# Chunked attention into a SwiGLU layer on one core: the second tile's tokens turned by VectorE and DMA instead of TensorE, weight stores and a tile's loads moved, 16 small transposes added

## The chip, the cores and the metric

The kernel runs on one core of a Trainium2 chip. Its time is the device time of one launch in microseconds (us); the number compared is the median of several runs. The core has TensorE (PE in the rows, with PEld for its weight loads), VectorE (DVE), ScalarE (ACT), GpSimd (POOL) and SyncE (SP), which here issues nearly all of the DMAs, one after the other.

## The reference

What is computed, cut to its core: attention inside chunks of 64 tokens for 8 batches and 8 heads, then RMS norm and a SwiGLU layer over the 4608 tokens, all in float32.

```python
scores = scale * (q_c @ k_c.T)            # chunks of 64, head_dim 64
attn = softmax(scores)                    # exp(s - max) / (sum + 1e-9)
x = (attn @ v_c)  -> (4608, 512)          # heads side by side
xn = x / sqrt(mean(x * x) + 1e-6) * rms_g
g, val = xn @ w_gate, xn @ w_val          # 512 -> 1536
out = (g * sigmoid(g) * val) @ w_out      # 1536 -> 512
```

## The kernel before, in words

**Tiles.** The 4608 tokens are 9 tiles of 512 (TT), each of two units of 256 tokens. Tiles 0 to 2 (PLAIN = 3) are computed plainly, the loop `for t in range(PLAIN)`. The other six go two at a time through `up_pair` and `down_pair`, which use a scheme with seven products on sums of weight blocks. Every operand of a product is split into a high and a low part (fp32r), and three products are summed (high by high, high by low, low by high): `up` is 12 matmuls of 128x512 for a gate (ps_g) and 12 for a value (ps_v), `down` is 12 into four accumulators (acc).

**A plain tile.** For each of the 12 blocks f of the hidden width: `gate_and_value(f)` on TensorE, `gated` (Silu on ScalarE, the product on VectorE, then the high and low parts gh and gl), and the `down` of block f-1. At the end come `down` of the last block and `evacuate`, which stores four blocks of rows.

**Weights.** During tile 0 ScalarE and VectorE turn the weights from their stored form into high and low parts (`conv_step`, lines 191 to 243), 18 pieces in all. These parts are written back to DRAM for the later tiles: blocks that are stored as they are by `save_plain` (lines 687 and 742, three stores of 512 KB into wsd and three of 256 KB into osd for each of six i), and sums of blocks by `sides` (loads `w<-wfd` at line 754, sums on GpSimd at 749, splits and stores at 777 to 780).

**The tokens of a tile.** A unit passes scores, softmax, product with v, and the norm, and gives rows of tokens. The layer wants them with the model's width on the partitions. Units 0 and 1 (tile 0) are turned in the prelude by TensorE transposes (`x_turn_unit`, line 544). Units 2 and 3 (tile 1) are computed during t == 0 (`norm_unit`) and turned by `x_transpose` at line 533: 16 transposes of 128x128 on TensorE, eight ahead of the last but one `down` of tile 0 and eight ahead of the last. From unit 4 on there is another way: `turn_x` swaps 32x32 blocks within partitions on VectorE (STREAM_TRANSPOSE, line 458) and writes the result to DRAM (away_x, line 461), and `turn_x_back` reads it back in four DMAs (line 468) so that it lands turned; `x_split` then scales by g and makes the parts xh and xl.

**What sets the order.** In the prelude the order of TensorE, ScalarE and VectorE is that of the code (`manual_schedule`), and TensorE's is that of the code from t == 1 on. Everything else, SP's queue of DMAs among it, is ordered by a scheduler. Each engine works off its queue in order, so a DMA that waits holds up the ones behind it in SP's queue. The DMAs named below are `qt`, `kt`, `vt` (a unit's inputs), `away_e` and `eT` (a unit's attention weights, out to DRAM and back turned), `away_x` and `x`.

**Line numbers.** They are those of the kernel before; in the changed one the same lines stand a few numbers off.

Of the kernel before, what the change touches and what calls it, by code (L numbers as in the profile page):

```python
# [13 lines left out]
AF = mybir.ActivationFunctionType  # L14
ALU = mybir.AluOpType
AX = mybir.AxisListType

P = 128
# [67 lines left out]
def tile_chunk_attn_swiglu(  # L86
# [47 lines left out]
    def bank(pool, name):  # L134
        return pool.tile([P, 512], F32, tag=pool_tag[id(pool)], name=name)
# [358 lines left out]
        nc.scalar.activation(spent, xs, AF.Square, accum_out=ss)  # L494
        return root(ss, "ri")

    def norm_unit(u, banks):
        rs = state.pop(("rs", u))
        subs = [state.pop(2 * u + s) for s in range(2)]
        first = 2 * u % NSUB  # L500
        xu = x[:, first : first + 2]
        xv = xu.rearrange("p s (j b a d) -> p j s b a d", j=2, b=2, d=Q)
        for j in range(2):
            for b in range(2):
                nc.vector.tensor_tensor(
                    xv[:, j, :, b],
                    banks[j].rearrange("p s (a b d) -> p b s a d", b=2, d=Q)[:, b],
                    rs[:, :, :, j].broadcast_to([P, 2, NPAIR, Q]),
                    op=ALU.mult,
                )  # L510
        ss = small.tile([P, 2], F32, name="ss_u")
        for s, st in enumerate(subs):
            spent = st["e"].rearrange("p a j k -> p (a j k)")
            nc.scalar.activation(spent, xu[:, s], AF.Square, accum_out=ss[:, s : s + 1])
        ri = root(ss, "ri_u")
        for s in range(2):
            nc.gpsimd.tensor_scalar(xu[:, s], xu[:, s], ri[:, s : s + 1], None, op0=ALU.mult)

    def x_split(dt, pt, cols):
        g = g_col[:, dt : dt + 1]  # L520
# [5 lines left out]
            lo, pt, g, hi.bitcast(F32), op0=ALU.mult, op1=ALU.subtract  # L526
        )

    def x_transpose(dts):
        for dt in dts:  # L530
            pt = bank(ps_a, "ps_x")
            for s in range(NSUB):
                nc.tensor.transpose(
                    pt[:, s * P : (s + 1) * P], x[:, s, dt * P : (dt + 1) * P], ident
                )
            x_split(dt, pt, slice(0, TT))

    def x_turn_unit(u, d, pool):
        pt = state["xt", u, d] = bank(pool, "ps_x")
        for k in range(2):  # L540
            for s in range(2):
                at = (2 * k + s) * P
                src = x[:, 2 * u + s, (d + k) * P : (d + k + 1) * P]
                nc.tensor.transpose(pt[:, at : at + P], src, ident)
# [600 lines left out]
    with tc.manual_schedule(engines=FIRST_IN_ORDER):  # L1145
        for i, pool in enumerate((ps_a, ps_h)):
            scores(i, two_banks(pool, "ps_s"))
        softmax(0)
        softmax(1)
        att_transpose(0)  # L1150
        conv_abs(0)
        att_transpose(1)
        conv_low(0)
        softmax_sum(0)
        softmax_sum(1)
        conv_clamp(0)
        for i, pool in enumerate((ps_h, ps_acc)):
            att_values(i, two_banks(pool, "ps_o"))
            first_norm(i)
        first_squares(0)  # L1160
        first_root(0)
        for i, pool in ((2, ps_acc), (3, ps_h)):
            scores(i, two_banks(pool, "ps_s"))
        softmax(2)
        scale_one = first_scale(0, False)
        next(scale_one)
        softmax(3)
        att_transpose(2)
        conv_low(1)
        conv_load(AHEAD)  # L1170
        att_transpose(3)
        next(scale_one)
        conv_abs(1)
        softmax_sum(2)
        conv_shift(0)
        softmax_sum(3)
        for i in (2, 3):
            att_values(i, two_banks(ps_acc, "ps_o"))
            first_norm(i)
        first_squares(1)  # L1180
        first_root(1)
        for d in range(0, NDT, 2):
            x_turn_unit(0, d, ps_a)
        conv_sign(0)
        conv_cast(0)
        conv_clamp(1)
        conv_shift(1)
        conv_load(AHEAD + 1)
        for _ in first_scale(1, True):
            pass  # L1190
        conv_end(0)
        for d in range(0, NDT, 2):
            x_turn_unit(1, d, ps_acc)
        for d in range(0, NDT, 2):
            for u in range(2):
                x_high_unit(u, d)
        for d in range(0, NDT, 2):
            for u in range(2):
                x_low_unit(u, d)
        conv_sign(1)  # L1200
        conv_abs(2)
        conv_cast(1)
        conv_low(2)
        conv_clamp(2)
        conv_end(1)
        between = [
            lambda: conv_shift(2),
            lambda: conv_abs(3),
            lambda: conv_sign(2),
        ]  # L1210
        gs = {0: gated(0, (0, 1, 2), lambda: between.pop(0)())}
        ps = {1: gate_and_value(1)}
        conv_load(AHEAD + 2)
        conv_cast(2)
        conv_low(3)
        conv_clamp(3)
        conv_end(2)
        conv_shift(3)
        conv_sign(3)
    conv_at[0] = EARLY  # L1220

    for t in range(PLAIN):
        if t == 1:
            ordered = tc.manual_schedule(engines={mybir.EngineType.PE})
# [2 lines left out]
            for n, u in enumerate((4, 5)):  # L1227
                for k, f in enumerate(unit_steps(u, x)):
                    at.setdefault(2 + 9 * n + FIRST_STEPS[k], []).append(f)
            half = Steps(at)  # L1230
            st = last.open("st", 1)
            made = [[] for _ in range(NF + 2)]
# [5 lines left out]
        elif t == 2:  # L1238
# [2 lines left out]
            at = {}  # L1241
            for n, u in enumerate(range(2 * PLAIN, 2 * PLAIN + 4)):
                for k, f in enumerate(unit_steps(u, (x, x2)[n // 2])):
                    after_it = {1: LATE_STEPS, 2: LONG_STEPS}.get(n, UNIT_STEPS)
                    at.setdefault(max(UNIT_AT[n] + after_it[k], 0), []).append(f)
            for i in range(OUT_FIRST):
# [15 lines left out]
        for f in range(NF):  # L1262
            if f in gs:
                conv_step()
                g = gs.pop(f)
            else:
                g = gated(f, CONVS[f % 2], conv_step, ps.pop(f, None))
            if t == 0:
# [10 lines left out]
                elif f in (2, 7):  # L1279
                    for i in (2 * u, 2 * u + 1):  # L1280
                        att_transpose(i)
                elif f in (3, 8):
                    o = two_banks(ps_a, "ps_o")
                    for i in (2 * u, 2 * u + 1):
                        att_values(i, o)
                    norm_unit(u, o)
                if f == NF - 1:
                    x_transpose((0, 1))
            elif t == 1 and f == NF - 1:
                for dt in range(NDT):  # L1290
                    x_split(dt, blocks(x)[:, :, dt], slice(0, TT))
            if t == 1:
                if f % 2 == 0:
                    save_plain(f // 2)
                for todo in made.pop(0):
                    todo()
            if t:
# [3 lines left out]
            if t:  # L1301
                half()
            prev = g
        if t == 0:
            x_transpose((2, 3))
        down(acc, NF - 1, *prev)
        for s in range(NSUB):
            evacuate(acc, t, s)
# [84 lines left out]
```

## Time and profile before

| | |
|---|---|
| median of 3 runs | 898.38 us (897.68 to 898.59) |
| the profiled execution | 898.29 us, its span 896.5 us |
| TensorE busy | 880.0 us, 98% of the span |
| VectorE, ScalarE, GpSimd busy | 607.6, 454.1, 185.7 us (68%, 51%, 21%) |
| granted TensorE clock, mean | 0.991 of full |
| DMA | 231.84 MB, mean 259 GB/s |

The span runs from the first to the last instruction; 1.8 us of the execution lie around it. The prelude takes the first 27 us, tile 0 ends at about 138 us, tile 1 at 242 us and tile 2 at 352 us. Times in the rows are microseconds from the span's start.

### The profile page before, as it was taken

The numbers are of one execution on the slowest core, as the hardware profiler recorded it, in microseconds if no ns is written. First come the engines' busy times: TensorE is split into PE (matmuls) and PEld (weight loads), VectorE is DVE, ScalarE is ACT, GpSimd is POOL, SyncE is SP. The second block draws the span as 40 slices with busy tenths as digits, with TensorE's granted clock in tenths as the row PEclk, the third lists the DMA queues.
The fourth block names the chain that finished last, engine by engine and source line by source line (L and its number), as shares of the span: only waits on it lengthen the run. The fifth ranks groups of instructions, "written<-read, shape, count | busy, mean of one in ns | idle before, by whom it ended". The sixth has DMA issues, their size and how long they took to land.

```text
span 896.5 us, 17443 instructions
## 1 busy us (share of the span) xinstructions
PE 880.0 (98%) x6828; PEld 720.6 (80%) x6828; DVE 607.6 (68%) x965; ACT 454.1 (51%) x772; POOL 185.7 (21%) x157
## 2 busy tenths in 40 slices
PE   5999999999999999999999999999999999999998
PEld 4778888888888888888887888888878888888886
DVE  6999955364568745985677997556769953334776
ACT  5988934253446464454456645435547522222452
POOL 0004050342200000233233003333330014323200
PEclk8899999999999999999999999999999999999999
DMA  9889999777978855698977877677667794445442
GB/s 349 328 318 336 332 337 347 239 255 235 303 252 234 267 170 196 250 298 294 320 240 265 318 301 286 245 277 249 232 231 286 281 355 171 152 154 199 179 165 95
DMA packets 85794, 231.84 MB, mean 259 GB/s; under 512 B 8912, under 2 KB 45264, under 8 KB 71504
## 3 DMA queue, kind: packets, MB, share of 16 engines
q1 hardware_dynamic: 84656, 230.20, 73.1%
q8 instruction: 54, 0.88, 0.4%
q10 hardware_dynamic: 1056, 0.52, 0.2%
q14 instruction: 28, 0.23, 0.1%
HBM read 167.25 MB, written 63.44 MB: 257 GB/s over the span
## 4 chain that ended last, share of the span: by engine, by line
PE 94%; DVE 2%; ACT 2%; DMA 0%; issue 0%; POOL 0%; ACTq 0%; DVEq 0%
PE ps_b L857 11%; PE ps_a L857 11%; PE ps_c L857 11%; PE acc L664 11%; PE ps_g L627 11%; PE ps_v L627 10%; PE ps_b L1070 6%; PE ps_c L1070 6%; PE ps_d L857 5%; PE ps_a L1070 5%; PE ps_d L1070 3%; PE ps_o L426 2%; PE ps_s L299 2%; PE ps_o L484 1%; DMA x<-qT_dram 0%; ACT raw L196 0%
## 5 line engine op out<-in xcount | busy, mean ns | idle before, releaser
L857 PE MATMUL ps_b<-xp,wr 128*128 128x512 f32 x432 | 104.7, 391 | 0.1
L857 PE MATMUL ps_c<-xp,wr 128*128 128x512 f32 x432 | 104.0, 390 | 0.0
L857 PE MATMUL ps_a<-xp,wr 128*128 128x512 f32 x432 | 103.8, 390 | 0.0
L627 PE MATMUL ps_g<-xh,parts 128*128 128x512 f32 x288 | 97.2, 399 | 0.1
L857 PEld LDWEIGHTS ps_b<-xp,wr 128*128 128x128 f32 x432 | 80.5, 188 | 17.4 <-issue 0.5
L857 PEld LDWEIGHTS ps_c<-xp,wr 128*128 128x128 f32 x432 | 80.9, 188 | 16.9
L627 PE MATMUL ps_v<-xh,parts 128*128 128x512 f32 x288 | 94.5, 389 | 0.0
L857 PEld LDWEIGHTS ps_a<-xp,wr 128*128 128x128 f32 x432 | 80.8, 188 | 17.0
L664 PE MATMUL acc<-parts,gh 128*128 128x512 f32 x288 | 90.2, 394 | 0.0
L945 POOL TENSOR_TENSOR g<-u,u 128x512 f32<-128x512 f32 x18 | 23.2, 1289 | 251.9 <-DVE u L941 141.3
L627 PEld LDWEIGHTS ps_g<-xh,parts 128*128 128x128 f32 x288 | 54.7, 190 | 12.7 <-ACT parts L237 0.6
L627 PEld LDWEIGHTS ps_v<-xh,parts 128*128 128x128 f32 x288 | 54.1, 188 | 11.2
L977 ACT CAST gh<-g 128x512 fp32r<-128x512 f32 x72 | 43.6, 622 | 37.8 <-PE ps_c L1070 13.5
L664 PEld LDWEIGHTS acc<-parts,gh 128*128 128x128 f32 x288 | 53.1, 188 | 11.3
L982 DVE TENSOR_TENSOR gl<-g,gh 128x512 fp32r<-128x512 f32 x72 | 49.3, 692 | 16.2 <-PE ps_a L1070 5.7
L913 ACT ACTIVATE p<-p 128x512 f32<-128x512 f32 x36 | 22.7, 632 | 70.0 <-POOL p L935 60.4
L935 POOL TENSOR_TENSOR p<-p,p 128x512 f32<-128x512 f32 x36 | 46.9, 1313 | 53.9 <-DVE rs L387 35.6
L627 PE MATMUL ps_g<-xl,parts 128*128 128x512 f32 x144 | 56.8, 395 | 0.1
L664 PE MATMUL acc<-parts,gl 128*128 128x512 f32 x144 | 56.1, 390 | 0.0
L627 PE MATMUL ps_v<-xl,parts 128*128 128x512 f32 x144 | 56.0, 389 | 0.0
L922 DVE TENSOR_TENSOR u<-ps_b,p 128x512 f32<-128x512 f32 x36 | 24.6, 687 | 41.5 <-PE ps_b L857 38.0
L857 PE MATMUL ps_d<-xp,wr 128*128 128x512 f32 x216 | 52.3, 391 | 0.0
(151 smaller groups left out, 1706.7 us busy)
## 6 DMA issues: line engine op xcount, KB each, us to landing
wr<-wsd SPq DMA_DIRECT2D x63, 1024.0 KB, 7.0
wo<-osd SPq DMA_DIRECT2D x30, 1024.0 KB, 7.6
raw<-w_up_dram SPq DMA_DIRECT2D x12, 1024.0 KB, 9.5
vt<-v_dram SPq DMA_DIRECT2D x18, 512.0 KB, 7.2
wsd<-parts SPq DMA_DIRECT2D x18, 512.0 KB, 8.3
qt<-qT_dram SPq DMA_DIRECT2D x17, 512.0 KB, 5.6
kt<-kT_dram SPq DMA_DIRECT2D x17, 512.0 KB, 6.6
away_e<-e SPq DMA_DIRECT2D x28, 256.0 KB, 3.5
```

What stands on the lines that cost most here:

```text
L299: nc.tensor.matmul(st["s"][j][c * CH : (c + 1) * CH, pr], st["q"][rows, pr, tok : tok + CH], st["k"][rows, pr, tok : tok + CH], start=True ...
L426: nc.tensor.matmul(st["o"][(2 * c + t) * Q : (2 * c + t + 1) * Q, h * D : (h + 1) * D], eT[c][rows, t, h], vt[rows, c, h], start=True, sto ...
L627: nc.tensor.matmul(ps, a[f][:, cols], b[dt], start=(dt == 0 and i == 0), stop=(dt == NDT - 1 and i == 2),)
L664: nc.tensor.matmul(acc[s], a[:, cols], b, start=(f == 0 and i == 0), stop=(f == NF - 1 and i == 2),)
L857: nc.tensor.matmul(ps, w[:, a, m, cols], xp[:, b, kt], start=start and kt == 0 and i == 0, stop=stop and kt == 1 and i == 2, skip_group_ch ...
L913: nc.scalar.activation(t, t if src is None else src, AF.Silu)
L922: nc.vector.tensor_tensor(kp["u2"], b["b"], kp["p1"], op=add)
L935: nc.gpsimd.tensor_tensor(kp["p5"], kp["p1"], kp["p5"], op=add)
L945: nc.gpsimd.tensor_tensor(g[:, 0, 1], kp["u2"], kept[0]["u2"], op=mult)
L977: nc.scalar.copy(gh, src)
L982: nc.vector.tensor_tensor(gl, src, pair[0].bitcast(F32), op=ALU.subtract)
L1070: nc.tensor.matmul(banks[m][name], w[:, (0, 1, 0)[k], m * P : (m + 1) * P], (gh, gh, gl)[k], start=opens and i == 0 and k == 0, stop=not ( ...
```

## The change

Four things are changed.

1. Units 2 and 3 are turned as the later units are. `norm_unit` writes its rows into x in the layout that `turn_x` wants; for unit 3 (`shared`) the scaling by the root moves from GpSimd to ScalarE. `turn_x` and `turn_x_back` are called in t == 0 for unit 2 at f = 7 and 8 and for unit 3 at f = 10. `x_transpose` is gone, and `next_tokens` splits tile 1's tokens out of x at the last f, with ScalarE and VectorE in the order of the code there.
2. `save_plain` is called for f = 0 to 5 of t == 1, once each, and no longer at every second f.
3. The loads of unit 6, the first of tile 3, are called in t == 1 beside the turn of unit 5 and no longer at the start of t == 2.
4. In the prelude `x_turn_unit(1, 0, ...)` gets 16 transposes of 64x64 of the identity ahead of its own, into the PSUM bank that it then overwrites.

The host's order of the output rows follows (tile 1's rows are turned as well).

```diff
-    def norm_unit(u, banks):
+    def norm_unit(u, banks, shared):
...
-        first = 2 * u % NSUB
-        xu = x[:, first : first + 2]
-        xv = xu.rearrange("p s (j b a d) -> p j s b a d", j=2, b=2, d=Q)
+        xu = x[:, 2 * u % NSUB : 2 * u % NSUB + 2].rearrange("p s c -> p (s c)")
+        xu = state["xu", u] = xu.rearrange("p (q a s d) -> p q a s d", q=4, a=NDT, s=2)
+        xv = xu.rearrange("p q (j b) s d -> p j s b q d", b=2)
+        xs = xu.rearrange("p q a s d -> p s (q a) d")
...
-            nc.gpsimd.tensor_scalar(xu[:, s], xu[:, s], ri[:, s : s + 1], None, op0=ALU.mult)
+            if shared:
+                nc.scalar.mul(xs[:, s], xs[:, s], ri[:, s : s + 1])
+            else:
+                nc.gpsimd.tensor_scalar(xs[:, s], xs[:, s], ri[:, s : s + 1], None, op0=ALU.mult)
...
-    def x_transpose(dts):
...
-    def x_turn_unit(u, d, pool):
+    def x_turn_unit(u, d, pool, spare=0):
         pt = state["xt", u, d] = bank(pool, "ps_x")
+        for _ in range(spare):
+            nc.tensor.transpose(pt[:CH, :CH], ident[:CH, :CH], ident[:CH, :CH])
...
-            x_turn_unit(1, d, ps_acc)
+            x_turn_unit(1, d, ps_acc, 16 if d == 0 else 0)
...
+    def next_tokens():
+        for dt in range(NDT):
+            x_split(dt, blocks(x)[:, :, dt], slice(0, TT))
...
+            at[2 + 9 + FIRST_STEPS[7]].append(lambda: load_unit(2 * PLAIN))
...
+                    if n == k == 0:
+                        continue
...
+            elif t == 0 and f == NF - 1:
+                ps_last = gate_and_value(f)
+                with tc.manual_schedule(engines={mybir.EngineType.Activation, mybir.EngineType.DVE}):
+                    g = gated(f, CONVS[f % 2], conv_step, ps_last)
+                    next_tokens()
...
-                    norm_unit(u, o)
-                if f == NF - 1:
-                    x_transpose((0, 1))
+                    norm_unit(u, o, u == 3)
+                if f in (7, 10):
+                    turn_x(2 + (f == 10))
+                if f in (8, 10):
+                    turn_x_back(2 + (f == 10), x)
...
-                if f % 2 == 0:
-                    save_plain(f // 2)
+                if f < NPR:
+                    save_plain(f)
...
-        if t == 0:
-            x_transpose((2, 3))
```

The order that results, at three places. The first is TensorE at the end of tile 0, from the last value block (ps_v) on, through the last but one `down` (the first acc rows) to the beginning of the last. Before:

```order
L627 MATMUL ps_v<-xl_126,parts 128x512
L627 MATMUL ps_v<-xh_122,parts 128x512
L533 MATMUL ps_x<-ident,x 128x128 x8
L664 MATMUL acc_566<-parts,gh 128x512 x2
L664 MATMUL acc_566<-parts,gl 128x512
...
L664 MATMUL acc_569<-parts,gh 128x512 x2
L664 MATMUL acc_569<-parts,gl 128x512
L533 MATMUL ps_x<-ident,x 128x128 x8
L664 MATMUL acc_566<-parts,gh 128x512 x2
L664 MATMUL acc_566<-parts,gl 128x512
```

And in the changed kernel:

```order
L624 MATMUL ps_v<-xl_126,parts 128x512
L624 MATMUL ps_v<-xh_122,parts 128x512
L661 MATMUL acc_582<-parts,gh 128x512 x2
L661 MATMUL acc_582<-parts,gl 128x512
...
L661 MATMUL acc_585<-parts,gh 128x512 x2
L661 MATMUL acc_585<-parts,gl 128x512
L661 MATMUL acc_582<-parts,gh 128x512 x2
L661 MATMUL acc_582<-parts,gl 128x512
```

The two groups of eight transposes (ps_x) are gone and nothing takes their place. The second place is TensorE at the end of the prelude, from the product with v (ps_o) over the turn of units 0 and 1 (ps_x) to the first gate. Before:

```order
L484 MATMUL ps_o_412<-vt,eT 64x64 x2
L484 MATMUL ps_o_413<-vt,eT 64x64 x2
L544 MATMUL ps_x<-ident,x 128x128 x16
L627 MATMUL ps_g<-xh_119,parts 128x512
L627 MATMUL ps_g<-xl_123,parts 128x512
```

And in the changed kernel:

```order
L484 MATMUL ps_o_412<-vt,eT 64x64 x2
L484 MATMUL ps_o_413<-vt,eT 64x64 x2
L541 MATMUL ps_x<-ident,x 128x128 x8
L536 MATMUL ps_x<-ident 64x64 x16
L541 MATMUL ps_x<-ident,x 128x128 x8
L624 MATMUL ps_g<-xh_119,parts 128x512
L624 MATMUL ps_g<-xl_123,parts 128x512
```

The 16 small ones stand between unit 0's eight transposes and unit 1's. The third place is SP's queue in tile 1, from the last store of the second group of sums to the inputs of unit 5 (qt, kt, vt). Before:

```order
L778 DMA wsd_145<-side 128x512
L780 DMA wsd_145<-w 128x2x256
L754 DMA w<-wfd_133 128x1024
L754 DMA w<-wfd_134 128x1024
L267 DMA qt<-qT_dram 128x1024
L268 DMA kt<-kT_dram 128x1024
L269 DMA vt<-v_dram 128x1024
```

And in the changed kernel:

```order
L775 DMA wsd_145<-side 128x512
L777 DMA wsd_145<-w 128x2x256
L751 DMA w<-wfd_133 128x1024
L684 DMA wsd_154<-parts 128x4x256
L684 DMA wsd_155<-parts 128x4x256
L684 DMA wsd_157<-parts 128x4x256
L739 DMA osd_162<-parts 128x2x256
L739 DMA osd_165<-parts 128x2x256
L739 DMA osd_171<-parts 128x2x256
L267 DMA qt<-qT_dram 128x1024
L268 DMA kt<-kT_dram 128x1024
L269 DMA vt<-v_dram 128x1024
```

One set of six plain stores (the fifth) now stands ahead of unit 5's inputs, and the load of wfd_134 has gone behind them. Before, all plain stores stood ahead of the first side stores in this queue.

## Rows read from the trace of the kernel before

**Rows 1.** The page, part 4: shares of the chain that ended last.

```profile
PE 94%; DVE 2%; ACT 2%; DMA 0%; issue 0%; POOL 0%; ACTq 0%; DVEq 0%
```

**Rows 2.** Waits of PE, whole span: total us, times, longest.

```profile
PE ps_s L299 <- DMA x<-qT_dram: 5.6, 2, 5.1
...
PE ps_x L544 <- ACT x L590: 2.0, 1, 2.0
```

**Rows 3.** The chain that ended last, in order: start us, us, what; 30 to 47 us.

```profile
30.20 1.14 DVE w L217
...
31.36 1.05 ACT parts L237
...
45.15 0.95 ACT parts L237
...
46.14 0.73 PE ps_g L627 x2
```

**Rows 4.** The same chain further on, to the end of tile 0.

```profile
99.94 2.72 PE ps_g L627 x12
...
117.58 2.72 PE ps_g L627 x12
...
131.18 0.87 PE ps_x L533 x8
132.06 2.74 PE acc L664 x12
134.80 0.87 PE ps_x L533 x8
135.67 2.74 PE acc L664 x12
```

**Rows 5.** Timeline of PE in the prelude: start us, us, line, operation, count [idle before <-releaser].

```profile
8.67 1.09 PE L357 MATMUL ps_t<-ident,e 128*128 128x128 f32 x4 [0.78 <-issue]
...
16.91 0.66 PE L357 MATMUL ps_t<-ident,e 128*128 128x128 f32 x4 [2.02 <-ACT e L316]
...
25.59 2.11 PE L544 MATMUL ps_x<-ident,x 128*128 128x128 f32 x8 [1.99 <-ACT x L590]
```

**Rows 6.** Windows: length, busy us (count) of PE, PEld, DVE, ACT, POOL; PEclk, DMA, GB/s.

```profile
18.00:31.00 13.00, 10.36 (x91) 8.14 (x92) 12.77 (x25) 12.21 (x23) 1.07 (x1) 0.50 0.96 372
```

**Rows 7.** Timelines of DVE, POOL, ACT and DVE: single operations.

```profile
96.19 1.22 DVE L243 TENSOR_TENSOR parts<-w,parts 128x1024 fp32r<-128x1024 f32 x1
...
113.30 1.15 POOL L151 TENSOR_TENSOR ri_u<-ss_u,mhalf 128x2 f32<-128x2 f32 x1 [28.04 <-ACT ss_u L150]
...
225.17 1.34 ACT L452 ACTIVATE xu<-xu,ri 128x512 f32<-128x512 f32 x2 [0.52 <-POOL ri L151]
...
226.54 1.25 DVE L458 STREAM_TRANSPOSE xu<-xu 128x1024 f32<-128x1024 f32 x1 [2.90 <-ACT xu L452]
```

**Rows 8.** DMA issues: count, KB each, median us from issue to landing.

```profile
wsd<-parts SPq DMA_DIRECT2D x18, 512.0 KB, 8.3
...
away_x<-xu SPq DMA_DIRECT2D x14, 512.0 KB, 3.0
x<-away_x SPq DMA_DIRECT2D x56, 128.0 KB, 4.3
```

**Rows 9.** Timeline of SP's queue: DMA issues merged by line.

```profile
139.50 2.43 SPq L687 DMA_DIRECT2D wsd<-parts  x3
141.98 3.93 SPq L742 DMA_DIRECT2D osd<-parts  x3
...
174.49 0.99 SPq L267 DMA_DIRECT2D qt<-qT_dram  x1
...
207.63 5.02 SPq L409 DMA_DIRECT2D eT<-away_e  x8
```

**Rows 10.** Timeline of PE in tile 1: unit 5's scores and its product with v.

```profile
187.53 1.16 PE L299 MATMUL ps_s<-kt,qt 64*64 64x64 f32 x64
...
218.78 1.48 PE L426 MATMUL ps_o<-vt,eT 64*32 64x64 f32 x128
```

More of the change, by code (lines that the diff above doesn't have):

```diff
@@ L512, in norm_unit @@
         for s, st in enumerate(subs):
-            spent = st["e"].rearrange("p a j k -> p (a j k)")
-            nc.scalar.activation(spent, xu[:, s], AF.Square, accum_out=ss[:, s : s + 1])
+            spent = st["e"].rearrange("p a j k -> p (a j) k").rearrange("p a (b d) -> p (a b) d", d=Q)
+            nc.scalar.activation(spent, xs[:, s], AF.Square, accum_out=ss[:, s : s + 1])
         ri = root(ss, "ri_u")
         for s in range(2):
-            nc.gpsimd.tensor_scalar(xu[:, s], xu[:, s], ri[:, s : s + 1], None, op0=ALU.mult)
+            if shared:
+                nc.scalar.mul(xs[:, s], xs[:, s], ri[:, s : s + 1])
+            else:
+                nc.gpsimd.tensor_scalar(xs[:, s], xs[:, s], ri[:, s : s + 1], None, op0=ALU.mult)
     def x_split(dt, pt, cols):
@@ L527, in x_split @@
         )
-    def x_transpose(dts):
[L530 to L536, printed above, removed]
-    def x_turn_unit(u, d, pool):
+    def x_turn_unit(u, d, pool, spare=0):
         pt = state["xt", u, d] = bank(pool, "ps_x")
+        for _ in range(spare):
+            nc.tensor.transpose(pt[:CH, :CH], ident[:CH, :CH], ident[:CH, :CH])
         for k in range(2):
@@ L1285, in tile_chunk_attn_swiglu @@
                         att_values(i, o)
-                    norm_unit(u, o)
-                if f == NF - 1:
-                    x_transpose((0, 1))
+                    norm_unit(u, o, u == 3)
[3 more added lines that the diff above has]
+                    turn_x_back(2 + (f == 10), x)
             elif t == 1 and f == NF - 1:
-                for dt in range(NDT):
-                    x_split(dt, blocks(x)[:, :, dt], slice(0, TT))
+                next_tokens()
             if t == 1:
-                if f % 2 == 0:
-                    save_plain(f // 2)
+                if f < NPR:
+                    save_plain(f)
                 for todo in made.pop(0):
@@ L1390 @@
     rows = np.concatenate([rows[: PLAIN * TT], pairs])
-    turned = rows[2 * TT :].reshape(-1, 4, 2, Q, DM).transpose(0, 2, 1, 3, 4).reshape(-1, DM)
-    return np.concatenate([rows[: 2 * TT], turned])
+    turned = rows[TT:].reshape(-1, 4, 2, Q, DM).transpose(0, 2, 1, 3, 4).reshape(-1, DM)
+    return np.concatenate([rows[:TT], turned])
```

## The prediction

> **What bounds the kernel now.** I read the chain of work first. TensorE holds 94% of it [rows 1], so time is TensorE's own work plus whatever makes TensorE wait. Then its waits: the long ones are the arrival of the first inputs (5.6 us) and one wait of 2.0 us for ScalarE in front of unit 1's transposes [rows 2]; both lie in the prelude, and no row names a wait inside tiles 0 to 2 worth half a microsecond. So after the prelude an instruction taken off TensorE shortens the run by its whole duration, and faster stores, loads, VectorE, ScalarE or GpSimd bring nothing unless TensorE waits for them.
>
> The prelude is another matter. There the chain, followed in order of time, lies on VectorE up to 31.34 us and on ScalarE from 31.36 to 46.1 us; only at 46.14 does it go over to TensorE, at the third gate block [rows 3]. What TensorE does faster between 22 and 46 us therefore ends in a longer wait, not in an earlier end. This decides what the 16 spare transposes are worth.
>
> **The 16 transposes that go.** At the end of tile 0 the chain shows two groups of eight, 0.87 us each, and each lengthens the `down` behind it from 2.72 to 2.74 us [rows 4]. TensorE was streaming before and behind them, so they cost 2 x (0.87 + 0.02) = 1.78 us, and the order shows nothing in their place: minus 1.78 us.
>
> **What turns the tokens instead.** VectorE gets two block transposes of 1.25 us [rows 7], at f = 7 and at f = 9 to 10. In that part of tile 0 it converts weights ahead of TensorE. The piece nearest to its use behind the first of them is done at 96.19 + 1.22 = 97.41 and wanted at 99.94 [rows 4, 7]: 2.5 us, of which 1.3 remain. For unit 3 the scaling moves to ScalarE, about 1.34 us for two rows of tokens, and that is an added wait: ScalarE stands in it until GpSimd's root is there, 113.30 + 1.15 = 114.45 [rows 7], with the Silu of block 9 queued behind. Scale done at 115.8, Silu (taken as long as one such operation, 0.67) at 116.5; block 10's gate wants the bank at 117.58 [rows 4]. 1.1 us remain. Cost: nothing, and up to about 1 us if either estimate is short by twice its margin.
>
> Then the way through DRAM for unit 3: VectorE's transpose ends at about 117.1, away_x lands after 3.0, the four reads back take some 2.5 us to issue (as the eight eT issues, 5.02 us for eight) and land after 4.3 [rows 8, 9]: 127 us. The splits can't begin before the last value block ends, 131.18 [rows 4], since they overwrite what it reads; TensorE wants the first result only after two `down`s, 131.2 + 5.4 = 136.6. The data have 4 us in hand to the first bound and 9 to the second. Tile 1 ends in the same way already, with splits straight from x behind the last gate, and no row of the waits stands there [rows 2]. Cost: nothing. GpSimd loses two scalings, of which nobody was waiting.
>
> **The stores and loads that move.** Called sooner in the code, the plain stores nevertheless come out later in SP's queue than some work that they preceded: unit 3's away_x and its reads stand where four sets of six stood, and the fifth set stands ahead of unit 5's qt and kt. Six stores hold SP for 2.43 + 3.93 = 6.4 us [rows 9]. Today qt is issued at 174.49 and unit 5's scores start at 187.53 [rows 9, 10]; in the changed kernel they start 1.78 earlier, 185.75. At the far end nothing is regained: qt at 174.49 - 1.78 + 6.4 = 179.1, kt 0.4 later, landing after 8.3 (the slowest kind of 512 KB in rows 8): 187.8, and TensorE waits 2.1 us. At the near end the queue reaches the six early, because a w load that waits for its buffer has gone behind qt; if that gives back 2.1 us or more, the cost is zero. I take zero, since 8.3 is for stores in the fullest stretch, and keep 2.1 for the range. Behind that, unit 5's eT reads are issued from 207.63 on for 5.02 us and land at about 217.0 (4.3 as the other small reads), wanted at 218.78, now 217.0 [rows 8 to 10]. Even if they don't move earlier at all, they are just in time; they wait for splits that ScalarE makes at TensorE's pace, so they should move. Unit 6's loads, sooner, feed nothing that waits today: zero.
>
> **The 16 spare transposes.** They stand where TensorE is idle for 1.99 us ahead of unit 1's transposes [rows 5]. The trace has no 64x64 transpose; the nearest row is eight of 128x128 at 2.11 us, 0.26 each [rows 5]. Between nothing and 16 x 0.26 = 4.2 us, I take half a column count, half a price: 2.1 us, which fills the gap and overruns it by 0.1. At 4.2 us they would push unit 1's transposes, and the chain behind them, by up to 2.2 us.
>
> What they might change is the clock: it is granted at 0.50, 1.2 GHz, from 18 to 31 us [rows 6], and at full rate afterwards. If it came back when the spares have closed the gap, TensorE's work from 25.6 to 31 us would take half as long, 2.7 us less. But by rows 3 VectorE and ScalarE set the end of that stage. I take zero.
>
> The sum: 898.29 - 1.78 = 896.51 for the profiled execution, which lies 0.09 below the median; for the median 898.38 - 1.78 = **896.6 us**, a gain of 0.198%. A measurement of this kernel can tell about 0.2% from no change, so the forecast lies on the line between "faster" and "same": 896.58 is the line.
>
> **The rivals.**
>
> *The clock's gain reaches the end.* If the reading of rows 3 is wrong and TensorE's pace before 46 us counts, up to 2.7 us more go: 893.9 at the far end, 895.2 with half of it. For it: TensorE is ready hardly earlier than ScalarE at 46.14, so the two run close. Against it: the chain there is unbroken on the two other engines, and their order is unchanged in the prelude. The Trainium skill (TensorE: Matmul & The Clock Gate, Part 4: PE-mode transpose) goes further: transposes do not count as busy, so the full clock does not engage for them. By that rule the spares would leave the clock as it is and this rival falls, at 896.6. The trace does not bear the rule out in that strictness: the same four transposes take 1.09 us at 8.67 and 0.66 us at 16.91 [rows 5], though between them the code has only transposes and products of 64 columns. Chance 0.09.
>
> *A small stall.* Unit 5's inputs, or one of the covers above, are late by less than 2.1 us: 897 to 898.7. Chance 0.10. *The spares cost more than the gap*: 897 to 898.8, chance 0.05.
>
> *Slower.* Unit 5's inputs come so late behind the plain stores that more is lost than gained. The place is TensorE at 185.75, the scores of unit 5. If the six stores take SP half as long again, 9.5 us, in a stretch where side stores use the DMAs too, qt goes at 182.2, kt lands at 190.9, and TensorE stands 5.2 us: 901.8. It decides from a wait of 3.6 us on (gain given back plus 0.2%), that is from kt landing after 189.4. For it: nothing else in SP's queue may overtake. Against it: today's inputs have several us in hand there. Chance 0.06.
>
> *It does not do what it says*: x arrives after 136.6 and the turn costs TensorE what the transposes cost, 898.4. It would need 9 us more than worked out. Chance 0.02.
>
> **How the numbers follow.** The forecast, no new wait worth naming, has 0.68, and its own range is 895.9 to 897.3 (the runs before spread by 0.9 us). Half of it lies under 896.58. Faster by over 0.2%: 0.34 + 0.09 = 0.43. Slower: 0.06, and 0.01 for what is left out. Same: 0.50. For 8 in 10 the range goes from half the clock's gain, 895.3, to most of the small stalls, 898.1.
>
> **What the profile would show.** Right: the two ps_x groups are gone, the last value block is followed at once by 24 acc matmuls and the next gate, with no wait of TensorE for ScalarE, VectorE or a DMA there; the 2.0 us wait in front of unit 1's transposes is shorter; the third gate block still starts at about 46.1 us whatever the clock did; every row of TensorE behind 140 us comes 1.8 us earlier. Wrong: a wait of the scores at about 186 us for qt or kt (the queue), of the product with v at 217 for eT, of a gate at 100 or 118 for VectorE or ScalarE, or a third gate block that starts clearly before 46 us, which would mean that the prelude is not bound as rows 3 say.

## The result, and the profile after

The changed kernel takes 903.54 us (median of 6 runs, 901.11 to 905.13); the kernel before, run beside it, 898.56 (6 runs, 897.68 to 899.40). The ratio is 1.0055, with a 95% interval of 1.0040 to 1.0071: slower by 5.0 us, where 896.6 and at most 898.1 were forecast. The profiled execution took 903.4 us, its span 901.6.

TensorE's share of the chain that ended last falls from 94% to 80%, page part 4 (compare [rows 1]):

```profile
PE 80%; DMA 8%; DVE 4%; ACT 3%; POOL 2%; issue 2%; SPq 1%; ACTq 0%; DVEq 0%; POOLq 0%
```

The waits of TensorE over the whole span (total us, times, longest), compare [rows 2]:

```profile
PE ps_s L299 <- DMA x<-qT_dram: 5.7, 2, 5.1
...
PE ps_g L624 <- DVE parts L243: 2.0, 1, 2.0
PE acc L661 <- ACT gh L649: 1.9, 1, 1.9
...
PE ps_x L541 <- ACT x L587: 0.5, 1, 0.5
```

Two waits of some 2 us are new, for converted weights (`parts`) in tile 0 and for gh at the end of tile 1. Setting the start of every TensorE group of the two traces side by side gives where the time went, in us:

| stretch | against before |
|---|---|
| prelude, to the first value block | +0.6 |
| tile 0, value block of f = 6 (85.28 before, 89.53 after) and the group behind it | +3.8 |
| end of tile 0, the two groups of transposes | -0.80 and -0.99 |
| tile 1, at 197 and 220 | +0.9 |
| end of tile 1 (242.08 before, 248.10 after) | +2.7 |
| the rest, at 415, 537 and 656 | -0.8 |

The sum is 5.4; the spans differ by 5.1. The transposes pay what was forecast. The chain there, start, us and what (compare [rows 4]):

```profile
130.15 2.72 PE ps_g L624 x12
132.87 2.72 PE ps_v L624 x12
135.59 5.44 PE acc L661 x24
141.03 2.72 PE ps_g L624 x12
```

24 `down` matmuls follow the last value block at once, and tile 1's first gate follows them: the turn by VectorE and DMA comes in time.

**The loss in tile 0.** ScalarE, 66 to 74 us (start, us, line, operation, count [idle before <-releaser]):

```profile
68.44 0.57 ACT L644 ACTIVATE sg<-ps_g 128x512 f32<-128x512 f32 x1
72.71 1.13 ACT L191 ACTIVATE w<-raw 128x1024 f32<-128x1024 f32 x1 [3.70 <-DMA wfd<-w]
```

The conversion at L191 wants a `w` buffer back that the DMA `wfd<-w` reads. SP issued that one at 66.41, at its old place in the order, and it landed after 6.2 us; before, issued at 65.86, after 3.0. TensorE gets the piece late, and works on at half its pace for a while:

```profile
85.70 0.73 PE L624 MATMUL ps_g<-xh,parts 128*128 128x512 f32 x2 [2.01 <-DVE parts L243]
...
86.54 1.06 PE L624 MATMUL ps_g<-xh,parts 128*128 128x512 f32 x2
```

Two matmuls take 1.06 us instead of 0.62; the granted clock of 85 to 90 us is 0.66, between 1.00 and 1.00. So 2.0 us are the wait and some 1.7 the 1.2 GHz behind it.

**The loss in tile 1.** SP's queue, compare [rows 9], and GpSimd's third and last sums of w blocks:

```profile
174.30 2.80 SPq L684 DMA_DIRECT2D wsd<-parts  x3
177.14 3.80 SPq L739 DMA_DIRECT2D osd<-parts  x3
181.03 0.73 SPq L267 DMA_DIRECT2D qt<-qT_dram  x1
...
183.07 3.08 SPq L684 DMA_DIRECT2D wsd<-parts  x3
186.19 5.04 SPq L739 DMA_DIRECT2D osd<-parts  x3
```

```profile
205.41 6.05 POOL L746 TENSOR_TENSOR w<-w 128x512 f32<-128x512 f32 x4 [18.44 <-DMA w<-wfd]
...
236.78 5.72 POOL L746 TENSOR_TENSOR w<-w 128x512 f32<-128x512 f32 x4 [5.04 <-DVE gl L653]
```

In the kernel before the same two stand at

```profile
195.72 5.75 POOL L749 TENSOR_TENSOR w<-w 128x512 f32<-128x512 f32 x4 [12.17 <-DMA w<-wfd]
...
229.27 5.80 POOL L749 TENSOR_TENSOR w<-w 128x512 f32<-128x512 f32 x4 [3.61 <-DMA qt<-qT_dram]
```

Two sets of six plain stores now hold SP for 14.7 us between 174 and 191; the side stores and the w loads behind them are late, the third sums by 9.7 us, the last by 7.5 (TensorE itself is 2.6 to 3.5 us late in this stretch). The chain at the end of tile 1 shows the rest of the way: the w load of the last sums, issued at 231.25 and landed at 236.66 (before, 224.31 and 229.11), the sums, the cast of the side block on ScalarE, its subtraction on VectorE, and only then the product of the last gate and its gh:

```profile
231.25 0.50 DMA w<-wfd
231.75 5.03 issue
...
236.79 1.28 POOL w L746
...
239.52 1.31 POOL w L746
...
240.85 0.63 ACT side L774
...
241.51 1.07 DVE w L776
...
242.98 0.68 DVE w L776
243.66 0.61 DVE sg L648
...
244.30 0.62 ACT gh L649
...
244.97 3.29 PE acc L661 x12
```

### The profile page after: what moved, and what is told of

The parts are those of the page before. It is cut to its first block, busy times and chain, and to the rows that moved or that the text cites. A ratio compares the mean times of both kernels' runs of the same rounds, so it can differ in the third digit from the quotient of the medians.

```text
span 901.6 us, 17466 instructions
## 1 busy us (share of the span) xinstructions
PE 881.8 (98%) x6828; PEld 720.9 (80%) x6828; DVE 615.1 (68%) x967; ACT 455.9 (51%) x774; POOL 175.7 (19%) x155
## 4 chain that ended last, share of the span: by engine, by line
PE 80%; DMA 8%; DVE 4%; ACT 3%; POOL 2%; issue 2%; SPq 1%; ACTq 0%; DVEq 0%; POOLq 0%
PE ps_a L854 11%; PE ps_c L854 11%; PE ps_b L854 11%; PE ps_g L624 7%; PE acc L661 6%; PE ps_v L624 6%; PE ps_c L1067 5%; PE ps_b L1067 5%; PE ps_d L854 5%; PE ps_a L1067 5%; PE ps_d L1067 3%; DMA wsd<-parts 2%; PE ps_o L426 2%; PE ps_s L299 2%; POOL w L746 1%
## 5 line engine op out<-in xcount | busy, mean ns | idle before, releaser
L854 PEld LDWEIGHTS ps_c<-xp,wr 128*128 128x128 f32 x432 | 80.9, 188 | 16.9
L648 DVE TENSOR_TENSOR sg<-ps_v,sg 128x512 f32<-128x512 f32 x36 | 24.6, 684 | 42.0 <-PE ps_v L624 32.7
```

Source lines behind the costliest of these rows:

```text
L648: nc.vector.tensor_tensor(sg, pv, sg, op=ALU.mult)
L854: nc.tensor.matmul(ps, w[:, a, m, cols], xp[:, b, kt], start=start and kt == 0 and i == 0, stop=stop and kt == 1 and i == 2, skip_group_ch ...
```

## Experiments: undoing one part each

Theory Q: SP's queue makes tile 1 late. Theory S: the spares cause the loss in tile 0. Four kernels, each timed against the kernel before (898.7). The fences show the lines of each edit that matter; the rest is cut.

e1, the changed kernel without spares:

```diff
-            x_turn_unit(1, d, ps_acc, 16 if d == 0 else 0)
+            x_turn_unit(1, d, ps_acc)
```

> The changed kernel without the 16 spare transposes. In the changed kernel's trace TensorE loses 3.7 us in tile 0, at the value block at 86 us, behind a write of weights (wfd) that took 6.2 us to land instead of 3.0 and held up ScalarE's next conversion by 3.7 us, and 2.7 us more at the border of tiles 1 and 2. Theory S (the spares, or the clock that they bring up, shift the prelude and cause the first loss): the loss at 86 us goes, 903.5 - 3.7 = 899.8, and the 2.7 at the border stay. Theory Q (both losses come from SP's queue and its DMAs, the spares have no part in it): 903.5 within 0.6, and the 2.0 us gap ahead of unit 1's transposes is back without the third gate block starting later than 46.7.

909.79 us, 1.0122 (1.0096 to 1.0149). All the other engines have the order of the changed kernel. The loss in tile 0 is gone, as S has it, but the kernel is 6.3 us slower than with spares, which neither theory foresaw. New are two stalls in products with v, for which the trace shows no releaser ("issue"), in unit 7's the larger; TensorE, 416 to 431 us:

```profile
416.21 1.47 PE L426 MATMUL ps_o<-vt,eT 64*32 64x64 f32 x127
422.91 0.31 PE L426 MATMUL ps_o<-vt,eT 64*32 64x64 f32 x1 [5.24 <-issue]
423.15 5.49 PE L854 MATMUL ps_a<-xp,wr 128*128 128x512 f32 x12
```

The last of 128 matmuls waits 5.2 us, and the twelve behind it take 5.5 instead of 2.9, at a granted clock of 0.60 from 423 to 430. The second stall, at 670 to 673, costs 2.5.

e2, the kernel before with the 16 spares alone (the same line the other way round):

> The kernel before, with the 16 spare transposes added and nothing else. Theory S (the spares shift the prelude and so cause the loss in tile 0): 898.6 + 3.7 = 902.3, with the wait of TensorE at about 86 us. Theory Q (the losses belong to the DMA queue): the spares fill an idle gap ahead of a chain on VectorE and ScalarE, 898.6 within 0.5, and the third gate block starts at 46.1. A third possibility, that the spares bring the clock up early and this reaches the end: down to 898.6 - 2.7 = 895.9, with the third gate block before 46.

902.10 us, 1.0033 (1.0015 to 1.0051): S. TensorE waits 1.7 us for the same piece of `parts`, and the order of every other engine is that of the kernel before. That place is not all of it: the traced execution (903.5) loses 2.0 us there, 1.2 in the prelude and 2.1 between 250 and 321 us.

e3, the turn alone, and e4, all plain stores ahead of the sums' loads:

```diff
# e3: the spares, the cadence of save_plain and unit 6's loads as before
# e4
-                if f < NPR:
-                    save_plain(f)
+                if f == 0:
+                    for i in range(NPR):
+                        save_plain(i)
```

> Of the change only the turn of units 2 and 3 by VectorE and DMA; plain stores at every second block, unit 6's loads and the prelude as in the kernel before. Theory Q (the turn's own DMAs push the plain stores out of tile 0 into tile 1, among the loads that feed the sums on GpSimd, and this makes the side casts and so the last gate of tile 1 late): the 1.8 us are gained at the end of tile 0, and 3.3 us or more are lost from there to the border of tiles 1 and 2, as in the changed kernel or worse, since the last set of six stands still later here: 900.1 or more without the loss at 86 us, 903.8 or more with it. Rival N (the new place of the stores alone does it): without it the turn keeps its gain, 896.8. In tile 0 nothing of the turn is issued before 90 us, so if the loss at 86 us is here again it is not the work of the turn in front of it.

914.79 us, 1.0182 (1.0165 to 1.0200). The turn's 1.8 us are gained, there is no loss at 86 us, and 10.7 us are lost from the end of tile 0 into tile 2. But not where Q put it: the last sums start at 230.7, hardly late, and the wait is 4.8 us for unit 6's kt (at 254), which SP issues at 248 behind the last set of six. The stalls of e1 are here too (5.9 us).

> The changed kernel with all six calls of the plain stores at the first block of tile 1, so that in SP's queue they all stand ahead of the loads that feed the sums, as in the kernel before. Theory Q: the sums on GpSimd, the side casts and the last gate of tile 1 come in time again, the 2.7 us at the border of tiles 1 and 2 and the 0.9 shortly before it go: 903.5 - 2.7 to - 3.6 = 899.9 to 900.8 if the loss at 86 us stays, 896.2 to 897.1 without it. Rival V (the border is late because ScalarE and VectorE have more to do in tile 1, not because of the queue): 903.5 within 0.6, and the wait of 1.9 us for gh at 245 us is there again. At the far end: 36 stores in one piece hold up unit 4's inputs, a new wait of the scores in tile 1.

916.32 us, 1.0191 (1.0172 to 1.0210). As Q has it, no wait for gh is left at the end of tile 1, but the test is weak: TensorE reaches that place 15 us later, which gives the sums that much more time. The far end of the expectation came true as well, with 14.3 us of TensorE in front of unit 4's scores, whose kt stands behind the stores. So whoever comes behind those stores in SP's queue is late: unit 4's inputs, the sums, or unit 6's.

## Experiments: what the spares do

From the end of tile 0 on, TensorE has had 32 instructions fewer in e1 and e3 (16 transposes and their weight loads) than in the kernel before and the changed one; in e2 and the changed kernel it has 32 more ahead of tile 0's f = 6. The DMA view has a queue named "instruction", of the whole span of the changed kernel:

```profile
q8 instruction: 54, 0.88, 0.4%
```

54 packets of 16 KB for 13,656 matmuls and weight loads, one for about 253; with 224 more of them (e7, below) there are 55. The Trainium skill (Runtime: NRT & Kernel Launch, Instruction fetch mechanics) says that an engine's instructions are refilled in blocks of 16 KB over a DMA queue of its own; the trace agrees. It calls the cost mostly hidden; here it is not. In e1 no such packet moves between 398.4 and 420.5 us; the next one goes at 420.5 to 421.5 (DMA view of e1, 420 to 421 us), and TensorE goes on at 422.9:

```profile
q8 instruction: 1, 0.02, 6.0%
```

So it is everywhere. In all the traces TensorE has, after 40 us, twelve waits of over half a microsecond without a releaser (in e1, e2, e3, e7, e9 and e12), and each ends 1.2 to 1.5 us after the end of such a packet; of its other waits over 0.3 us none ends less than 4 us after one. The 128 matmuls of a product with v and their weight loads are 256 instructions, about as many as one packet brings, and run in 1.5 us.

This is theory F: a shift in the number of TensorE instructions moves the fetches, in tile 0 onto the write of wfd, in tile 3 to where a product with v outruns them. Theory C: the early clock or the closed gap in the prelude brings the loss in tile 0. Four more kernels:

```diff
# e5: after, the 16 at the head of TensorE's stream
+            pt = two_banks(pool, "ps_s")
+            for _ in range(0 if i else 16):
+                nc.tensor.transpose(pt[0][:CH, 0, :CH], ident[:CH, :CH], ident[:CH, :CH])
# e6: after, the 16 ahead of tile 0's last down; e7: before, 112 there
+        if t == 0:
+            pt = bank(ps_a, "ps_x")
+            for _ in range(16):
+                nc.tensor.transpose(pt[:CH, :CH], ident[:CH, :CH], ident[:CH, :CH])
# e9: before, 32 in the prelude
+            x_turn_unit(1, d, ps_acc, 32 if d == 0 else 0)
```

> The changed kernel with its 16 spare transposes at the very start of TensorE's stream, where it waits for the first inputs, and not ahead of unit 1's transposes. The number of TensorE instructions ahead of every later place is the same as in the changed kernel. Theory F (TensorE's instructions come in by DMA in blocks of 16 KB; the spares shift the block that is fetched in tile 0 from 75 us to 67 to 68 us, into the write of wfd, and this is the loss at 86 us): the fetch is at 67 to 68 again, wfd lands late again, and the value block at 86 us loses 2 to 4 us: 903.5 within 1.5. Theory C (the early clock in the prelude, or the closed gap, shifts the work and so causes that loss): the loss is gone, 899.8.

907.63 us, 1.0106 (1.0089 to 1.0123). It decides nothing: the scheduler put ScalarE's prelude in another order (a conversion stands 3.3 us for its raw weights ahead of unit 1's norm), so that the stretch in question isn't the same, and its fetch comes at 73.8 us.

> The changed kernel with its 16 spare transposes at the end of tile 0, ahead of the last down, so that TensorE has as many instructions as in the kernel before both up to there and from there on. Theory F: the fetch in tile 0 is at 74 to 75 us as before, wfd lands in 3 us and the loss at 86 us is gone; the stalls of 5 and 2 us in unit 7's product with v (413 to 428 us) and near 660 us, which the kernel without spares has, are gone too; what is left is the queue in tile 1: 898.6 - 1.8 + 0.3 (the spares) + 3 to 3.7 = 900.1 to 900.8. Theory C: as without spares, 909.8 less nothing, since the prelude is the same as there. If the stalls at 413 and 660 us come from the turn or the stores and not from the count of instructions, they stay, and the time is 907 or more.

904.12 us, 1.0073 (1.0050 to 1.0095). The fetch in tile 0 is back at 74 to 75 us and wfd lands in 3.0; the loss at 86 us and the stalls at 413 and 660 are gone, as F has it. The time missed the expectation of 900.1 to 900.8. The traced execution, at 907.9 the slowest of the four, shows more than the median lost: the spares took 1.1 us in place of 0.3, the clock came back late in the prelude (+1.4), unit 5's kt was late by 1.3, and a wait of 3.9 us for gh was followed by 1.2 GHz (granted clock 0.57 from 245 to 253 us).

> The kernel before with 112 spare transposes of 64x64 at the end of tile 0, and nothing else: 224 TensorE instructions more from there on, which is 32 short of a block of 256, as the kernel without spares is 32 short. Theory F: the spares cost about 2 us, and the product with v at 413 us and the one near 650 us stall by some 8 and 2 us as they do in the kernel without spares: 898.6 + 2 + 8 to 10 = 908 to 911, with waits of TensorE in them for which the trace shows no releaser. If those stalls belong to the turn or to the stores that move, this kernel has only the spares' cost: 900.6.

913.87 us, 1.0168 (1.0143 to 1.0193). This settles the stalls: nothing of the change is in this kernel, only 224 TensorE instructions (and a few operations of ScalarE, VectorE and SP that the scheduler put in another order in tile 1). They cost 6.4 us where they stand (I had taken 2), and then the stalls of e1 appear at the same products:

```profile
420.60 1.47 PE L426 MATMUL ps_o<-vt,eT 64*32 64x64 f32 x126
425.78 0.27 PE L426 MATMUL ps_o<-vt,eT 64*32 64x64 f32 x2 [3.72 <-issue]
425.98 4.61 PE L857 MATMUL ps_a<-xp,wr 128*128 128x512 f32 x12
```

With the slow matmuls behind them they cost 5.1 us there and 4.4 at 672 to 680, 9.5 of the 8 to 10 that F gave.

> The kernel before with 32 spare transposes in the prelude where e2 has 16; every other engine's order is that of the kernel before. Theory F (the fetch of a block of TensorE's instructions hits the write of wfd at 66 to 69.5 us): 16 spares moved the fetch from 75 to 68 us, 32 move it to about 64, ahead of that write, so wfd lands in 3 us again, the loss at 86 us is gone, and what is left is the time by which 32 spares overrun the gap, up to 1.5 us: 898.6 to 900.1, against 902.1 with 16. Theory C (the spares as such, by the early clock or the closed gap, bring that loss): it stays or grows, 902 or more.

908.05 us, 1.0105 (1.0076 to 1.0134). The loss at 86 us is gone with 32 spares where 16 bring it, against C. But the time is 8 us over what F gave, since F was only followed in tile 0: from there on the blocks stand at a third place, and TensorE stalls at 316 (3.8 us without a releaser), at 578 (2.2) and at 641 (1.6). And the fetch did not leave the write of wfd; it goes at 66 to 67 us, and only takes less time. The kernels whose engines have the same order up to there, the write of wfd being issued at 65.7 to 67.4 us:

| kernel | fetch near it, at us | took | wfd landed after | L191's wait | value block of f = 6 later by |
|---|---|---|---|---|---|
| before, e1, e3, e6, e7, e8, e10 | 74 to 77 | 0.9 to 1.8 | 3.0 | none for wfd | 0 |
| e9, e11, e12 | 66 to 68 | 1.0 | 3.9 to 4.0 | 1.4 to 1.5 | 0 |
| e4 | 67 to 68 | 1.6 | 4.6 | 2.1 (put down to VectorE) | 0.7 |
| e2 | 68 to 69 | 2.8 | 5.9 | 3.4 | 2.0 |
| after | 67 to 68 | 3.0 | 6.2 | 3.7 | 3.7 |

The rows of the fetch in the DMA view, windows of 1 us (packets, MB, share of 16 engines): the changed kernel from 67 us, then the kernel before from 74 us:

```profile
q8 instruction: 1, 0.02, 18.8%
```

```profile
q8 instruction: 1, 0.02, 7.0%
```

18.8% of 16 us are 3.0 us, 7.0% are 1.1. That the number of TensorE instructions ahead of that write makes the loss is shown (e1, e2, e6, e9). Its size is not fixed by it: the changed kernel, e2 and e4 have the same instructions up to there, and lose 3.7, 2.0 and 0.7 us in the one execution of each that was traced. The write and the packet end together: in all six traces with a packet beside it the write lands 2.1 us after the packet's end, and in the three that lose time TensorE gets its piece 13.1 us after the landing. That the packet holds up the write, and not some third thing both, is still only argued; e5, in its other order, has a write of 5.7 us without a fetch beside it.

## Experiments: another place for the stores

e12 is the changed kernel with 32 spares instead of 16 (the line of e9).

> The changed kernel with 32 spare transposes in the prelude instead of 16 and nothing else; every other engine's order is unchanged. In the runs so far ScalarE's wait for wfd in tile 0 grew with the time that the fetch of a block of TensorE's instructions took beside it: 3.0 us of fetch, 3.7 of wait; 2.8 and 3.4; 1.6 and 2.1; 1.0 and 1.5 with 32 spares, where TensorE lost nothing. Theory F: with 32 spares the fetch takes 1 us again, the loss of 3.7 at 86 us is gone, no stalls at 413 and 660 us (from tile 1 on the blocks stand as in e2 and e11), and the queue's loss of 3 to 3.5 us in tile 1 stays, perhaps with 1 us more in front of unit 5's scores, which the late tile 0 had covered: 899.8 to 901. If the loss at 86 us comes from the spares whatever the fetch does: 903.5 or more.

902.93 us, 1.0047 (1.0029 to 1.0066). The loss at 86 us is gone, 3.6 us, and the kernel is but 0.6 us faster. GpSimd's third and last sums, and the waits of TensorE from 210 to 252 us:

```profile
203.52 6.07 POOL L746 TENSOR_TENSOR w<-w 128x512 f32<-128x512 f32 x4 [20.08 <-DMA w<-wfd]
...
235.94 5.73 POOL L746 TENSOR_TENSOR w<-w 128x512 f32<-128x512 f32 x4 [6.11 <-DMA w<-wfd]
```

```profile
PE acc L661 <- ACT gh L649: 1.5, 1, 1.5
PE acc L661 <- issue: 1.0, 1, 1.0
PE ps_o L426 <- DMA eT<-away_e: 0.5, 1, 0.5
```

That is neither F's 899.8 to 901 nor the 903.5 of its rival. The sums stand within 2 us of those of the changed kernel although tile 0 ends 3.5 us sooner, and tile 2 starts at 248.74 instead of 248.10. But this execution, at 905.1, lies 2.1 us above its median, and not all that it loses in tile 1 is the queue's: the 1.0 us without a releaser comes behind an instruction packet, and after the wait for gh the twelve matmuls of the last `down` run at 1.2 GHz (245 to 249 us). Nor does the queue fix that time: in e1, whose other engines have the same order and whose tile 0 ends as early, the last sums start at 233.28 and tile 2 at 244.60, 3.5 us sooner than in the changed kernel. There the loss of tile 0 comes back in full (903.5 less 3.8, plus 10.1 for the stalls, is the 909.8 measured). Why e12 gets so little back is open. Each loss alone leaves the kernel slower than before (e2 has only the first, e12 only the second).

e8, e10 and e11 call the 18 stores of osd in tile 2. The scheduler still puts five or six of them between 174 and 197 us, the others from 247 us on; the last store of wsd, at 185 us in the changed kernel, comes at 160 to 173:

```diff
# e8: e6, and in the loop of the blocks; e10 and e11: f in range(6, 12), f - 6
+            if t == 2 and f % 2 == 0:
+                save_plain_out(f // 2)
# e10, e11: unit 5's qt and kt called ahead of its vt
+                        at.setdefault(6, []).append(lambda: load_qk(5))
+                        f = lambda: load_v(5)
# e10: 16 matmuls of 32 columns at the end of tile 0; e11: 32 transposes in the prelude
```

> The kernel of e6 with the plain stores of w_out's parts (osd, 18 of the 36) called in tile 2 at every second block; the stores of wsd stay in tile 1. The osd parts are read from tile 3's down on only. Theory Q (SP's queue in tile 1 makes the sums and side casts late, and so the last gate of tile 1): the loads that feed the sums get free, the wait for gh at the border of tiles 1 and 2 and the 0.9 us before it go: 897 to 898, the 1.8 of the removed transposes less the spares' 0.3 and what the clock of the prelude does; osd stores still stand ahead of unit 5's inputs, so up to 2 us may be lost there. Rival V (the border is late because VectorE and ScalarE have more to do): no better than e6, 900 to 901.

900.24 us, 1.0014 (1.0003 to 1.0025), 3.9 less than e6 with only those calls moved, though not the 897 to 898 expected. The last sums, in e6 and here:

```profile
238.94 5.70 POOL L746 TENSOR_TENSOR w<-w 128x512 f32<-128x512 f32 x4 [7.19 <-DMA w<-wfd]
...
232.50 5.78 POOL L748 TENSOR_TENSOR w<-w 128x512 f32<-128x512 f32 x4 [3.57 <-DVE sg L648]
```

No wait of TensorE is left between 210 and 252: Q. Rival V, more work on ScalarE and VectorE, falls, since that work is the same. Five osd stores still stand ahead of unit 5's kt, and cost 1.0 us.

> A version meant to keep the gain: the turn; 16 spare matmuls of 32 columns at the end of tile 0 instead of the transposes in the prelude; the osd stores called in tile 2 from its seventh block on, one set for each block; unit 5's qt and kt loaded earlier than its vt. Theories F and Q together: no fetch in the write of wfd, no stall at 413 and 660 us, no wait for gh at the border, no wait for unit 5's kt (1.0 to 1.3 us in e6 and e8): 898.5 - 1.8 + 0.3 to 0.6 for the spares and up to 1.4 for the prelude's clock, which came back late in e6 and e8: 897 to 898.5. If the osd stores cost in tile 2 what they cost in tile 1: 900 or more.

899.38 us, 1.0015 (1.0001 to 1.0029), where 897 to 898.5 were expected. No wait in tile 1, no stalls; the matmuls came out as 32 and cost 2.1 us, more than the turn's gain, and the scores at 306 us wait 1.2 us for VectorE.

> The same version with 32 spare transposes in the prelude instead of the matmuls at the end of tile 0. Theory F: the fetch in tile 0 is ahead of the write of wfd as in e9, and from tile 1 on the blocks stand as in e2, without the stalls at 413 and 660 us: 898.5 - 1.8 + 0.5 to 1.5 of overrun in the prelude: 897.2 to 898.2. Theory C: the loss at 86 us is back, 900 or more.

897.74 us (10 runs), 0.9987 (0.9977 to 0.9996): 5.8 us faster than the changed kernel, and the only one below the kernel before, by 1 us, a difference at the edge of what can be measured. GpSimd's two sums are where they were before the change:

```profile
196.05 5.80 POOL L762 TENSOR_TENSOR w<-w 128x512 f32<-128x512 f32 x4 [13.52 <-DMA w<-wfd]
...
228.68 5.73 POOL L762 TENSOR_TENSOR w<-w 128x512 f32<-128x512 f32 x4 [4.02 <-DVE sg L662]
```

## Why the prediction was wrong

The sum put two terms at zero that cost 3.6 and 3.8 us in the traced execution, the stores and the spares; both are taken up below.

**The transposes that go: right.** 1.78 us were forecast, 1.79 measured.

**The turn: right.** No wait of TensorE for x or the splits at the end of tile 0 in the changed kernel, whose tile 0 is late, nor in e1, whose tile 0 is not; there unit 3's x lands at 128.5 for the 127 worked out. In e3 and e12 one of 0.2 to 0.3 us for xl.

**The stores and loads that move: the first step that failed.** Put at zero, they cost 3.6 us in tile 1 of the traced execution. The prediction saw that sets of six go behind other work and named their price for SP, 6.4 us each, but followed only two consumers behind them, unit 5's inputs and its eT. The first was sized well: up to 2.1 us, measured 1.3 in e6 and 1.0 in e8, and none in the changed kernel, where kt landed at 189.44 for scores at 190.15, nor in e1 and e12. The second, put at just in time, cost 0.6 in the changed kernel (the product with v at 222 us, whose last eT lands at 222.2) and 0.4 to 0.5 in e1 and e12. Not followed was the longest chain that hangs on that queue: the w loads that stand behind the stores, GpSimd's sums, the casts and subtractions, and with them the last gate's gh, which stands behind them on VectorE and ScalarE. GpSimd is busy for only 21% of the span, but the chain that passes through it did not have the time in hand to start its last sums 7.5 us later. The "slower" rival was the right mechanism at the wrong place, and so got 0.06; of the places that the prediction named as signs of being wrong (186, 217, 100 or 118 us) only the product with v shows a loss, those 0.6 us.

**The spares: right in the prelude, and the second step that failed.** They took 1.52 us (2.1 estimated), and the gap shrank to 0.55; compare [rows 5]:

```profile
24.05 1.52 PE L536 MATMUL ps_x<-ident 64*64 64x64 f32 x16
26.11 1.33 PE L541 MATMUL ps_x<-ident,x 128*128 128x128 f32 x8 [0.55 <-ACT x L587]
```

The third gate block starts at 46.66, 0.5 later, and 0.5 late was the kernel already at 16.9, ahead of the spares. But "zero" left out that an instruction is also something to be fetched: the prediction priced the spares by the gap that they fill, and never by the 32 instructions by which they shift all that follows. With them where they are, tile 0 lost 3.7; and the 16 transposes that go are 32 instructions too, which without the spares would have cost 10 us in tiles 3 and on (e1). The prediction read no row for that. Unit 7's product with v, 1.92 us at 413.33 before the change and 1.48 after it, may be a small forerunner of the stalls; that isn't shown.

**The clock's gain: right.** Windows of the changed kernel (length, busy us of PE, PEld, DVE, ACT, POOL; granted clock, DMA, GB/s), compare [rows 6], and the last two of e11:

```profile
24.00:28.00 4.00, 3.31 (x26) 2.43 (x25) 3.96 (x7) 3.59 (x8) 1.09 (x1) 0.87 0.82 272
28.00:31.00 3.00, 2.30 (x6) 1.82 (x6) 3.00 (x8) 3.00 (x6) 0.00 (x0) 0.57 0.98 392
```

```profile
28.00:31.00 3.00, 2.44 (x10) 1.78 (x11) 3.00 (x8) 3.00 (x6) 0.00 (x0) 1.00 0.96 392
31.00:36.00 5.00, 4.05 (x34) 3.08 (x33) 3.87 (x5) 4.52 (x6) 0.00 (x0) 1.00 0.94 317
```

The clock rose early and fell again; e1, e6, e8 and e10, which have no spares there, show such a rise between 22 and 24 us too, so the rise is not the spares' work. With 32 spares it stayed at full (e9, e11, e12): the first value block then comes 0.8 to 1.3 us sooner, the second gate waits 0.9 to 1.0 us for ScalarE's Silu at 35.5, and nothing is left of it. The reading of [rows 3] holds. It holds one way only: in e2, e6 and e8 the clock came back later, and 1.2 to 1.6 us were lost and stayed lost. That differs by execution, not by kernel: the six kernels with the prelude of the kernel before (e1, e3, e6, e7, e8, e10) come to the third gate block 0.0 to 1.5 us later than it did. The Trainium skill (TensorE: Matmul & The Clock Gate, Part 4: PE-mode transpose) says that the full clock does not engage for transposes. The traces speak against it in that strictness: from 28 to 31 us the three kernels with 32 spares are granted 1.00, the eleven others 0.50 to 0.79. The row that the prediction set against it, four transposes at 8.67 and at 16.91 us, says nothing on it, since 128 ordinary matmuls lie between the two (11.35 to 14.9 us).

**The chances.** "Slower" had 0.07 because one route to it was priced; its 901.8 came near the measured 903.5 by luck, from a wait that did not occur. With 36 stores moved behind other work in a full queue, each consumer behind them was a route, and so was each shift in TensorE's instruction count.

## What to carry to other kernels

When DMAs change places in a queue, list everybody behind them to the next point where TensorE waits, and price the longest chain, not the nearest. When TensorE instructions are added or removed ahead of dense stretches of small matmuls, look where the instruction queue's packets fall; a few spare instructions in an idle gap can be worth, or cost, more than the edit. And one traced execution is not the median: e6's lay 3.7 us above its own, e12's 2.1, so a loss read from one trace is to be confirmed by the time of a kernel without it.

## What the runs showed of the hardware

- TensorE's instructions come by DMA in 16 KB packets (54 for 13,656 of them, 55 for 13,880), and TensorE stood up to 5.2 us for one (e1). Twelve such waits in six traces each ended 1.2 to 1.5 us after a packet's end.
- A 512 KB write with such a packet beside it landed 2.1 us after the packet's end in six traces of six, 3.9 to 6.2 us after its issue in place of 3.0.
- A wait of 2.0 us at 84 us was followed by 1.2 GHz for a while (0.66 in 85 to 90), one of 1.7 in e2 at the same place was not (1.00). The 4.8 us of e3 were followed by 0.50 from 254 to 259.
- 112 transposes of 64x64 into one place of PSUM took 6.44 us at the full clock, 58 ns each (e7), and 32 matmuls of 64x32 into one place 2.05 us, 64 ns each (e10); the 128 matmuls of 64x32 of a product with v, which go to different places, took 1.48 us, 12 ns each. Which of the differences between them makes this was not tried.
